# A new written-out order for a fused attention and FFN kernel: half tiles of their own for sequences 0 and 1, and the last output tile in two column halves

## The chip, the core and the metric

The kernel runs on one core of a Trainium2 chip. The core has five engines with instruction queues of their own: TensorE (PE, matrix products, with weight loads shown as PEld), VectorE (DVE), ScalarE (ACT), GpSimd (POOL) and SyncE (SP). They run side by side and wait for each other by semaphores only. Loads from HBM are issued by POOL, stores and transposes by DMA by SP. The metric is the device time of one execution in microseconds; smaller is better.

## The reference

Eight sequences of 576 positions, eight heads of 64. Keys and values are averaged over groups of 8 positions (72 remain), attention runs over these, and a gated FFN with a convolution over three positions follows. Cut to what is computed:

```python
k_p = k.reshape(B, H, Sp, pool, D).mean(axis=3)          # pool 8: 576 -> 72
v_p = v.reshape(B, H, Sp, pool, D).mean(axis=3)
scores = scale * np.matmul(q, k_p.transpose(0, 1, 3, 2))
scores = scores - np.max(scores, axis=-1, keepdims=True)
attn = np.exp(scores)
attn = attn / (np.sum(attn, axis=-1, keepdims=True) + 1e-09)
x = np.matmul(attn, v_p)  # -> (8, 576, 512), heads side by side
h = np.maximum(x @ w_in, 0.0)                            # 512 -> 1024
conv_out[s] = sum(conv_w[k] * h[s + k - 1] for k in range(3))
gate = 1.0 / (1.0 + np.exp(-conv_out))
out = (h * gate) @ w_out                                 # 1024 -> 512, float32
```

## The kernel before

The sequences are paired into four groups, [0, 1], [2, 3], [4, 5], [6, 7]. A sequence's 576 positions are 4 tiles of 128 and a half tile of 64. A group therefore has nine attention tiles: t = 0 to 3 of its first sequence, t = 5 to 8 of its second, and t = 4, whose 128 rows are the two half tiles together (`parts`, L479). So t = 4 needs keys, queries and values of both sequences, and both FFNs need t = 4 (`need`, L1045).

An attention tile passes through these steps: scores on PE (`att_scores`), the maximum over each head on DVE (`att_max`, L529), its subtraction (`att_shift`: for group 0 two PE matmuls into the same PSUM banks, L549; for the others a DVE addition, L541), the exponential on ACT (L567), the transpose of the exponentials (groups 0 and 1: five PE transposes, L578, and a copy, L592; groups 2 and 3: `att_send`, a DMA transpose issued by SP), the product with the values on PE (`att_values`, L603), the division on DVE (`att_divide`, L616 and L618), and the transpose into xT (groups 0 and 1 by PE and a copy, L635 and L643; groups 2 and 3 by a DMA transpose from SP, `att_out`).

The FFN of a sequence: eight blocks of 128 features through w_in (`ffn_in`, two halves of four matmuls each, L648) with a relu on ACT (L657); sequence 0 alone goes tile by tile (`ffn_in_tile`, L669). Then four convolutions of two blocks each, as products with diagonal matrices in quarters of the array (`ffn_conv`, L730, 64 or 80 matmuls), a tanh on ACT (L741), the gate on DVE (L752 to L759). Nine output tiles per group (`ffn_out`, L764, two steps of four matmuls of 512 columns), each copied out of PSUM (`ffn_copy`, L775) by DVE or ACT and stored by two DMAs of 64 rows (`ffn_store`, L787).

Before the attention of a sequence its q, k and v are loaded by POOL (`load_q`, L251; `load_k`, L251; `load_pair`, L258; `load_v`, L269 and L272), keys are pooled and queries transposed on PE, values pooled on DVE. Constants are made at the start: the pooling matrix (cleared by DVE, L310 to L312, cut out by POOL, L299, doubled by DVE, L315), the identity, the head mask (POOL, L318 and L320), its wide form (DVE, L337), cleared buffers (DVE, L295), and the first Exp, which brings ACT's table in (`start_exp`, L290 and L291). PE runs matmuls on a blank tile ("fills", L367) where the order has a spare.

Each such step is an operation of a graph (`add`) with the engines that can do it, what it comes after, and the buffers ("tokens") that it uses. The numbers given to `add` (durations, keys, landing times, counts) served a planner and emit nothing. What runs is the written order: `order` (L138) goes through ORDER, where n // 2 names the operation and n % 2 the engine, −1 is a fill, FORMS picks the array form (full, halves or quarters) and PLACES the PSUM banks. The other buffers are handed out in rotation (L149 to L151):

```python
                elif k.slots is None:
                    i = taken[k.ring] = taken.get(k.ring, -1) + 1
                    k.slots = [i % self.rings[k.ring]]
```

Every engine's queue holds its operations in that order.

Of the kernel before, what the change touches and what calls it, by code (L numbers as in the profile page):

```python
# [12 lines left out]
ACT = mybir.ActivationFunctionType  # L13
# [20 lines left out]
class Graph:  # L34
# [20 lines left out]
    X_DMA = 4  # L55
    SHIFT_DVE = 1
# [53 lines left out]
    )  # L110
    FORMS = (
        0, 0, 1, 1, 0, 1, 1, 1, 0, 0, 0, 0, 0, 1, 1, 0, 1, 0, 0, 0, 0, 0, 0, 0, 0, 1, 0, 0, 0, 1, 0, 1, 0, 1, 1, 1, 1, 1, 1, 1,
        0, 0, 0, 0, 0, 0, 0, 0, 1, 0, 1, 0,
    )
    PLACES = (
# [22 lines left out]
    def order(self):  # L138
        forms, places, spares, taken, done, seen = iter(self.FORMS), iter(self.PLACES), list(self.spares), {}, [], set()
        for n in self.ORDER:  # L140
# [4 lines left out]
            for k in o.uses:  # L145
# [14 lines left out]
def kernel(  # L160
# [10 lines left out]
    nc = tc.nc  # L171
# [985 lines left out]
```

## Time and profile before

| | us |
|---|---|
| median of 3 runs | 236.06 (235.92 to 236.71) |
| the profiled execution | 237.85 |
| its span, first to last instruction | 235.6 |
| PE busy in the span | 216.2 |
| DVE busy | 173.9 |
| ACT busy | 146.3 |
| POOL busy | 28.0 |
| mean granted TensorE clock | 0.98 of full speed |

The span is what the profile shows; the execution's own time is 2.25 longer. A busy share is a mean over stages, and the stages differ: loads at the start, attention and FFN mixed in the middle, output matmuls at the end. Groups of instructions are written as line, engine, operation, output<-inputs, count, busy time, mean duration, and idle time ahead of them with what ended it.

### The profile page before, as it was taken

What the parts mean: (1) busy time and instruction counts of PE and PEld (TensorE: products, weight loads), DVE (VectorE), ACT (ScalarE), POOL (GpSimd) and SP (SyncE); (2) the same over time, 40 slices, a digit from 0 to 9 for tenths busy, and PEclk for the clock granted to TensorE, in tenths of its full rate; (3) what the DMA queues carried; (4) which work ended last, traced back from release to release, by engine and by line L of the source; (5) the groups of instructions that cost most, each with busy time, mean ns of one, the idle gap of its engine ahead of it and who ended that gap; (6) DMA issues with size and microseconds to landing.
All of it is one profiled execution on the core that took longest, in us unless ns stands there. A gap on an engine that the chain in (4) does not pass through costs nothing. (4 is left out here: it accounts for less than half of the span.)

```text
span 235.6 us, 7790 instructions
## 1 busy us (share of the span) xinstructions
PE 216.2 (92%) x3362; PEld 150.8 (64%) x3362; DVE 173.9 (74%) x365; ACT 146.3 (62%) x246; POOL 28.0 (12%) x45
## 2 busy tenths in 40 slices
PE   6697899969999899988998899899999999999991
PEld 2455799756678777556764477568766665875440
DVE  4489886996999999988799779769757625716510
ACT  2245668896888997749766576358434563685320
POOL 7930731110000520300000000000000000000000
PEclk9979999997999999999999999999999999999998
DMA  5999999999940299999135777656665642601596
GB/s 88 163 186 207 207 207 207 207 207 206 191 98 3 19 199 185 230 179 171 25 70 32 155 150 137 130 124 132 91 133 116 130 85 46 136 3 38 112 203 143
DMA packets 44006, 31.51 MB, mean 134 GB/s; under 512 B 23596, under 2 KB 39364, under 8 KB 43972
## 3 DMA queue, kind: packets, MB, share of 16 engines
q0 software_dynamic: 16288, 16.26, 42.9%
q1 hardware_dynamic: 27604, 14.64, 32.3%
q8 instruction: 26, 0.43, 0.8%
q10 hardware_dynamic: 80, 0.13, 0.1%
q14 instruction: 8, 0.07, 0.1%
HBM read 32.52 MB, written 9.44 MB: 178 GB/s over the span
## 5 line engine op out<-in xcount | busy, mean ns | idle before, releaser
L764 PE MATMUL psum<-w_out_sb,gT 128*128 128x512 bf16 x288 | 70.2, 382 | 0.0
L648 PE MATMUL psum<-xT,w_in_sb 128*128 128x288 bf16 x448 | 63.7, 286 | 2.3 <-ACT tg L741 2.3
L648 PEld LDWEIGHTS <-w_in_sb 128*128 128x128 bf16 x448 | 42.0, 98 | 16.5 <-issue 2.8
L657 ACT ACTIVATE hT<-psum 128x576 bf16<-128x576 f32 x56 | 35.0, 649 | 23.8 <-PE psum L648 23.6
L741 ACT ACTIVATE tg<-psum 128x576 bf16<-128x576 f32 x64 | 37.5, 652 | 12.5 <-PE psum L730 11.0
L764 PEld LDWEIGHTS <-gT 128*128 128x128 bf16 x288 | 27.0, 98 | 25.4 <-issue 0.7
L529 DVE TENSOR_REDUCE negm<-psum 128x8 f32<-128x576 f32 (+1 forms) x36 | 27.1, 752 | 5.8 <-PE psum L516 3.9
L730 PE MATMUL psum<-hT,dw 64*64 64x288 bf16 (+4 forms) x1152 | 30.3, 246 | 1.1 <-ACT eT L592 0.3
L730 PEld LDWEIGHTS <-dw 64*64 64x64 bf16 x1152 | 25.3, 107 | 8.0 <-issue 7.3
L618 DVE TENSOR_TENSOR x<-psum,r 128x512 bf16<-128x512 f32 x36 | 24.9, 692 | 1.2
L775 ACT COPY osb<-psum 128x512 f32<-128x512 f32 (+1 forms) x26 | 14.6, 581 | 16.9 <-PE psum L764 15.1
L759 DVE TENSOR_TENSOR gT<-gT,hT 128x1152 bf16<-128x1152 bf16 x32 | 24.3, 758 | 1.1
L567 ACT ACTIVATE e<-sd 128x576 bf16<-128x576 f32 x27 | 18.2, 684 | 7.9 <-DVE sd L541 4.9
L775 DVE COPY osb<-psum 128x512 f32<-128x512 f32 (+1 forms) x11 | 7.3, 667 | 19.9 <-PE psum L764 14.5
L541 DVE TENSOR_TENSOR sd<-psum,negm 128x576 f32<-128x576 f32 x27 | 20.4, 755 | 0.8
L755 DVE TENSOR_SCALAR gT<-tg 64x576 bf16<-64x576 bf16 x64 | 19.7, 309 | 1.5 <-ACT tg L741 0.2
L603 PE MATMUL psum<-vm,eT 128*128 128x130 bf16 (+5 forms) x240 | 18.4, 222 | 1.4 <-DVE negm L529 1.4
L752 DVE TENSOR_SCALAR gT<-tg 128x576 bf16<-128x576 bf16 x32 | 9.5, 305 | 11.7 <-ACT tg L741 11.6
L603 PEld LDWEIGHTS <-eT 128*128 128x128 bf16 (+1 forms) x240 | 14.5, 100 | 4.3 <-DMA eT<-e 1.5
L434 DVE TENSOR_TENSOR v<-v 128x1280 bf16<-128x1280 bf16 (+2 forms) x24 | 13.0, 542 | 0.2
L592 ACT COPY eT<-psum 128x640 bf16<-128x640 bf16 x15 | 10.3, 691 | 4.4 <-PE psum L578 4.1
L616 DVE RECIPROCAL r<-psum 128x8 f32<-128x8 f32 x36 | 7.3, 202 | 7.8 <-PE psum L603 7.6
(73 smaller groups left out, 205.9 us busy)
## 6 DMA issues: line engine op xcount, KB each, us to landing
out_dram<-osb SPq DMA_DIRECT2D x71, 128.0 KB, 2.4
v<-in_v_dram POOLq DMA_DIRECT2D x8, 512.0 KB, 18.5
qp<-in_q_dram POOLq DMA_DIRECT2D x7, 576.0 KB, 14.0
kk<-in_k_dram POOLq DMA_DIRECT2D x3, 1152.0 KB, 13.9
w_in_sb<-in_moe_w_in_dram POOLq DMA_DIRECT2D x2, 512.0 KB, 17.0
w_out_sb<-in_moe_w_out_dram POOLq DMA_DIRECT2D x1, 1024.0 KB, 20.0
kk<-in_k_dram POOLq DMA_DIRECT2D x2, 288.0 KB, 4.5
kk<-in_k_dram POOLq DMA_DIRECT2D x1, 576.0 KB, 12.8
```

Source lines behind the costliest of these rows:

```text
L529: nc.vector.tensor_reduce(out=a["m"][0:rows], in_=a["s"][0:rows, :, 0:2 * KW].rearrange("p a (h s) -> p a h s", s=Sp), axis=AX.X, op=OP.ma ...
L541: nc.vector.tensor_tensor(out=a["d"][0:rows], in0=a["s"][0:rows, :, 0:2 * KW].rearrange("p a (h s) -> p a h s", s=Sp), in1=a["m"][0:rows]. ...
L603: nc.tensor.matmul(out=a["o"][lo:hi, h // 4, (h % 4) * (D + 1):(h % 4 + x1 - x0) * (D + 1)], lhsT=a["eT"][:, j, lo:hi], rhs=buf("vm", b)[: ...
L618: nc.vector.tensor_tensor(out=a["x"][0:rows].rearrange("p (a h d) -> p a h d", a=2, d=D), in0=ov[:, :, :, 0:D], in1=r[0:rows].unsqueeze(3) ...
L648: nc.tensor.matmul(out=banks(ps)[:, j, 0:SC], lhsT=w_in_block(dc, fb), rhs=buf("xT", g)[:, dc, i * S + j * SC:i * S + (j + 1) * SC], start ...
L657: nc.scalar.activation(out=buf("hT", b)[:, fb, :].rearrange("p (a s) -> p a s", a=2), in_=banks(ps)[:, :, 0:SC], func=ACT.Relu, scale=0.5,)
L730: nc.tensor.matmul(out=banks(pss[r ^ c])[c * D:(c + 1) * D, j, lo:hi], lhsT=dw[r * D:(r + 1) * D, tap * n_fb + fb, :], rhs=hT[r * D:(r + 1 ...
L741: nc.scalar.activation(out=tg.rearrange("p (a s) -> p a s", a=2), in_=banks(ps)[:, :, 0:SC], func=ACT.Tanh, scale=0.5,)
L755: nc.vector.tensor_scalar(out=gate[r * D:(r + 1) * D, fb], in0=tg[(1 - r) * D:(2 - r) * D], scalar1=1.0, scalar2=None, op0=OP.add)
L759: nc.vector.tensor_tensor(out=gate[:, both], in0=gate[:, both], in1=buf("hT", b)[:, both], op=OP.mult)
L764: nc.tensor.matmul(out=bank(ps)[0:rows, :], lhsT=buf("gT", g)[:, fb, t * P:t * P + rows], rhs=w_out_sb[:, fb, :], start=(fb == 0), stop=(f ...
L775: copy(out=osb[0:rows, columns], in_=bank(ps)[0:rows, columns])
```

## The change

Group 0 is named in `APART`: its t = 4 is now the half tile of sequence 0 alone, and a new t = 9 is the half tile of sequence 1, written to its own columns of xT (`columns_of`). The FFN of sequence 0 needs tiles 0 to 4, that of sequence 1 tiles 5 to 9. Ten attention tiles instead of nine are run in group 0. Output tile t = 4 still has both halves.

The last output tile (sequence 7, t = 8) is computed in two column halves of eight matmuls of 256 columns, each into a PSUM bank of its own; each half is copied and stored by two DMAs of 64 rows by 256 columns as soon as it is there (the first half's both from SP, the second's from SP and ACT).

ORDER, FORMS and PLACES are replaced, and PLACES now names the buffers of all rings. Some of the planner's numbers change. Read out of the lists:

| stretch | before | after |
|---|---|---|
| POOL at the start | k of 0 (2 loads), identity, pooling matrix, q of 0 (2), q 1, v 0, k 1, head mask, q 2, w_in (2), v 1, k of 2 and 3, q 3, w_out, q 4, v 2, v 3, v 4, q 5, k of 4 and 5 | k of 0 (2), head mask, identity, pooling matrix, q of 0 (2), v 0, k 1, q 1, q 2, w_in first half, v 1, w_in second half, k of 2 and 3, q 3, q 4, w_out, v 2, v 3, v 4, k of 4 and 5, q 6, q 7, q 5 |
| fills | 17 ahead of the first keys, then 5 and 3 | 4 ahead of the first keys, then 1, 1 and 1 |
| `start_exp` | first on DVE and ACT | amid the attention of group 1 |
| mask columns, wide mask, pick matrix | behind the first maxima | ahead of the first maximum |
| convolutions of sequence 0 (pairs of blocks) | 2, 1, 3, 0, two query preparations between | 1, 0, 2, 3, two query preparations between |
| first output matmuls | (0, t=2), behind all of PE's attention work for sequence 1 | (0, t=1), ahead of the values of (0, t=5) and the transposes back of t = 5, 6, 7 |
| end of PE | ..., (3, 5) second step, (3, 8) first, (3, 8) second | ..., (3, 5) second step, (3, 4) first, half 0 of (3, 8), (3, 4) second, half 1 of (3, 8) |
| end of SP | (3, 6), (3, 4), (3, 7), (3, 5), one half of (3, 8) | (3, 6), (3, 7), (3, 5), half 0 of (3, 8) twice, (3, 4) twice, one store of half 1 |

The diff, cut:

```diff
+    APART = (0,)
...
     ORDER = (
...
-        forms, places, spares, taken, done, seen = iter(self.FORMS), iter(self.PLACES), list(self.spares), {}, [], set()
+        forms, places, spares, done, seen = iter(self.FORMS), iter(self.PLACES), list(self.spares), [], set()
...
-                if k.slots is None and k.ring == "ps":
+                if k.slots is None:
                     i = next(places)
                     k.slots = list(range(i, i + k.n))
-                elif k.slots is None:
-                    i = taken[k.ring] = taken.get(k.ring, -1) + 1
-                    k.slots = [i % self.rings[k.ring]]
...
+        if t == 4 and g in Graph.APART:
+            return [(0, TB, bs[0])]
         if t == 4:
             return [(i * TB, (i + 1) * TB, b) for i, b in enumerate(bs)]
-        return [(0, P, bs[1])]
+        return [(0, TB if t == 9 else P, bs[1])]
+
+    def columns_of(g, t):
+        first = 4 * P + TB if t == 9 else t * P
+        return slice(first, first + rows_of(g, t))
...
-            out=buf("xT", g)[:, :, t * P:t * P + rows], in_=att[g, t]["x"][0:rows, :]
+            out=buf("xT", g)[:, :, columns_of(g, t)], in_=att[g, t]["x"][0:rows, :]
...
+    def half_columns(x):
+        return slice(x * d_model // 2, (x + 1) * d_model // 2)
+
+    def ffn_out(g, t, fbs, ps, columns=slice(0, d_model)):
+        rows = P
+        for fb in fbs:
...
-                    out=out[b].rearrange("(p c) d -> c p d", c=C)[c],
-                    in_=osb[j * TB:(j + 1) * TB, :],
+                    out=out[b].rearrange("(p c) d -> c p d", c=C)[c, :, columns],
+                    in_=osb[j * TB:(j + 1) * TB, columns],
...
-    LATE = 2.0
+    LATE = 1.8
...
-    c1 = add({"DVE": 0.6}, soon(), clear_pool_matrix)
+    c1 = add({"DVE": 1.5}, soon(), clear_pool_matrix)
...
-            o = add({"SP": 1.29}, key, lambda: att_send(g, t), after=[o, ze], uses=[e, eT], land=(1.7, 0, 1))
+            o = add({"SP": 1.29}, key, lambda: att_send(g, t), after=[o, ze], uses=[e, eT], land=(2.1, 0, 1))
...
-        need = [xdone[g, t] for t in range(5)] if i == 0 else [xdone[g, t] for t in range(4, 9)]
+        need = [xdone[g, t] for t in (range(5) if i == 0 else range(5, 10) if g in Graph.APART else range(4, 9))]
...
+            if b == B - 1 and n == len(n_outs[b]) - 1:
+                o = None
+                for x in range(2):
+                    sm = token("ps")
+                    o = add(pe(*[P * 2] * 8), key + x, lambda t=t, x=x, sm=sm: ffn_out(g, t, range(n_fb), sm, half_columns(x)),
+                            after=need + [wout, o], uses=[sm, gtok[g]], mode=FULL, count=16)
+                    c = add(either(0.42, 0.38), key + x, None, after=[o], uses=[osb, sm])
+                    c.emit = lambda c=c, t=t, x=x, sm=sm: ffn_copy(g, t, sm, copier(c), half_columns(x))
+                    for r, (e, queue) in enumerate((("SP", nc.sync), ("ACT" if x else "SP", nc.scalar if x else nc.sync))):
+                        add({e: 0.59}, key + x, lambda t=t, x=x, r=r, queue=queue: ffn_store(g, t, queue, r, half_columns(x)),
+                            after=[c], uses=[osb], land=(2.0, 0, 1))
+                continue
...
-            if b == B - 1 and n == len(n_outs[b]) - 1:
-                o = [add(d, key, lambda t=t, sm=sm, x=x, copy=copy: ffn_copy(g, t, sm, copy, slice(x * P * 2, (x + 1) * P * 2)),
-                         after=[o], uses=[osb, sm])
-                     for x, (d, copy) in enumerate(((dve(0.4), nc.vector.tensor_copy), (act(0.4), nc.scalar.copy)))]
-                for x, (e, queue) in enumerate((("SP", nc.sync), ("ACT", nc.scalar))):
-                    add({e: 0.59}, key, lambda t=t, x=x, queue=queue: ffn_store(g, t, queue, x), after=o, uses=[osb], land=(2.0, 0, 1))
-                continue
```

More of the change, by code (lines that the diff above doesn't have):

```diff
@@ L642, in att_copy_out @@
         rows = rows_of(g, t)
-        copy(out=buf("xT", g)[:, :, t * P:t * P + rows], in_=att[g, t]["xps"][:, 0:n_dmc, 0:rows])
+        copy(out=buf("xT", g)[:, :, columns_of(g, t)], in_=att[g, t]["xps"][:, 0:n_dmc, 0:rows])
     def ffn_in(b, fb, j, ps):
@@ L759, in ffn_gate @@
         nc.vector.tensor_tensor(out=gate[:, both], in0=gate[:, both], in1=buf("hT", b)[:, both], op=OP.mult)
-    def ffn_out(g, t, j, ps):
-        rows = rows_of(g, t)
-        for fb in range(n_fb // 2 * j, n_fb // 2 * (j + 1)):
+    def half_columns(x):
[3 more added lines that the diff above has]
+        for fb in fbs:
             nc.tensor.matmul(
-                out=bank(ps)[0:rows, :],
+                out=bank(ps)[0:rows, columns],
                 lhsT=buf("gT", g)[:, fb, t * P:t * P + rows],
-                rhs=w_out_sb[:, fb, :],
+                rhs=w_out_sb[:, fb, columns],
                 start=(fb == 0),
@@ L772, in ffn_copy, with ffn_store @@
     def ffn_copy(g, t, ps, copy, columns=slice(0, d_model)):
-        rows = rows_of(g, t)
+        rows = P
         osb = buf("osb", g, t)
         copy(out=osb[0:rows, columns], in_=bank(ps)[0:rows, columns])
-    def ffn_store(g, t, queue, only=None):
+    def ffn_store(g, t, queue, only=None, columns=slice(0, d_model)):
         osb = buf("osb", g, t)
@@ L813 @@
     FULL, HALF, QUARTER = (128, 128), (128, 64), (64, 64)
-    n_tiles = {b: [t for t in range(9 if len(groups[g]) == 2 else 5) if (t < 5) == (i == 0)]
-               for b, (g, i) in where.items()}
+    n_tiles = {b: [t for t in range(10 if g in Graph.APART else 9) if (t < 5) == (i == 0)] for b, (g, i) in where.items()}
     n_outs = {b: list(range(5)) if len(groups[g]) == 1 else [t for t in range(9) if (t < 4) == (i == 0)]
@@ L891, in add_load_pair @@
         loads["kk", g] = add({"POOL": 0.65}, key, lambda: load_pair(g), uses=[kk[g]], land=(LATE, 2 * kb, RATE))
-    picked = add({"DVE": 0.5}, START + Graph.DW - 1, build_pick, after=[c0])
+    picked = add({"DVE": 0.95}, START + Graph.DW - 1, build_pick, after=[c0])
     for b in (1, 2, 3):
@@ L1027, in add_att @@
         if b0 >= Graph.X_DMA:
-            o = add({"SP": 1.29}, key, lambda: att_out(g, t), after=[o], uses=[x, xtok[g]], land=(1.7, 0, 1))
+            o = add({"SP": 1.29}, key, lambda: att_out(g, t), after=[o], uses=[x, xtok[g]], land=(2.1, 0, 1))
         else:
@@ L1083, in add_out @@
         for n, t in enumerate(n_outs[b]):
-            rows = rows_of(g, t)
             key = w + 3 * rounds[n] - 1 + Graph.OUT + (Graph.LAST if b == B - 2 else 0) if b < B - 1 else w + n
             key += nudge("ot", 9 * g + t)
-            sm, osb = token("ps"), token("osb", g, t)
+            osb = token("osb", g, t)
+            need = [a for x in groups[g][0:i + 1] for a in gdone[x]]
+            if b == B - 1 and n == len(n_outs[b]) - 1:
[10 more added lines that the diff above has]
+                continue
@@ L1088, in add_out @@
+            sm = token("ps")
             o = None
             for j in range(2):
-                need = [a for x in groups[g][0:i + 1] for a in gdone[x]]
-                o = add(pe(*[512] * 4), key, lambda t=t, j=j, sm=sm: ffn_out(g, t, j, sm), after=need + [wout, o],
-                        uses=[sm, gtok[g]], mode=FULL if rows == P else HALF, count=8)
-            if b == B - 1 and n == len(n_outs[b]) - 1:
-                o = [add(d, key, lambda t=t, sm=sm, x=x, copy=copy: ffn_copy(g, t, sm, copy, slice(x * P * 2, (x + 1) * P * 2)),
-                         after=[o], uses=[osb, sm])
-                     for x, (d, copy) in enumerate(((dve(0.4), nc.vector.tensor_copy), (act(0.4), nc.scalar.copy)))]
-                for x, (e, queue) in enumerate((("SP", nc.sync), ("ACT", nc.scalar))):
-                    add({e: 0.59}, key, lambda t=t, x=x, queue=queue: ffn_store(g, t, queue, x), after=o, uses=[osb], land=(2.0, 0, 1))
-                continue
+                o = add(pe(*[512] * 4), key, lambda t=t, j=j, sm=sm: ffn_out(g, t, range(4 * j, 4 * j + 4), sm), after=need + [wout, o],
+                        uses=[sm, gtok[g]], mode=FULL, count=8)
```

14 lines of the change are left out of this document (7 added, 7 removed), and 125 rows, old and new, of tables (ORDER, PLACES).

## The prediction

> **What bounds the kernel now.** I read the page's busy shares first, then stage by stage the table of windows, then what ends PE's idle times, and last the timeline around them and the tail.
>
> ```profile
> span 235.6 us, 7790 instructions
> PE 216.2 (92%) x3362; PEld 150.8 (64%) x3362; DVE 173.9 (74%) x365; ACT 146.3 (62%) x246; POOL 28.0 (12%) x45
> ```
>
> The windows (us, then each engine's busy time, TensorE's granted clock, DMA share, GB/s):
>
> ```profile
> 0.00:8.00 8.00, 6.18 (x49) 2.95 (x51) 2.42 (x13) 1.71 (x3) 6.75 (x15) 1.00 0.65 93
> 8.00:11.50 3.50, 1.95 (x35) 1.27 (x30) 2.17 (x8) 1.28 (x5) 3.36 (x7) 1.00 1.31 193
> 11.50:15.00 3.50, 3.06 (x26) 1.63 (x26) 3.46 (x12) 1.94 (x3) 2.18 (x4) 0.51 1.17 182
> 15.00:28.00 13.00, 10.38 (x276) 7.81 (x275) 11.78 (x21) 7.04 (x12) 3.97 (x6) 1.00 1.22 204
> ...
> 42.00:50.00 8.00, 7.23 (x231) 5.46 (x219) 7.71 (x18) 7.04 (x13) 0.76 (x1) 1.00 1.23 208
> 50.00:52.00 2.00, 0.40 (x6) 0.14 (x4) 1.89 (x7) 1.81 (x5) 1.01 (x1) 1.00 1.24 204
> 52.00:56.00 4.00, 4.00 (x49) 2.94 (x49) 2.22 (x3) 2.31 (x4) 0.00 (x0) 0.57 1.24 207
> 56.00:100.00 44.00, 42.90 (x686) 32.05 (x688) 42.23 (x79) 37.59 (x64) 6.46 (x9) 1.00 0.82 137
> 100.00:122.00 22.00, 20.07 (x413) 14.99 (x402) 19.44 (x45) 15.76 (x27) 0.00 (x0) 1.00 0.72 108
> 122.00:152.00 30.00, 27.46 (x384) 17.99 (x383) 25.31 (x45) 18.24 (x30) 0.00 (x0) 1.00 0.69 123
> 152.00:231.00 79.00, 78.77 (x984) 50.58 (x982) 44.71 (x99) 41.23 (x71) 0.00 (x0) 1.00 0.51 105
> ```
>
> From 152 us PE never rests: the time is settled earlier. Up to 28 us DVE sets the pace (11.78 of 13.0) with loads arriving at 204 GB/s; 42 to 52 is DVE and ACT; 56 to 100 has PE and DVE both above 95%. The dear stops of PE (the wait in brackets stands ahead of the named matmul; the first is followed by half clock, the 0.57 above), and the tail:
>
> ```profile
> 51.76 0.29 PE L635 MATMUL psum<-ident,x 128*128 128x128 bf16 x2 [1.60 <-issue]
> ...
> 106.90 0.28 PE L648 MATMUL psum<-xT,w_in_sb 128*128 128x288 bf16 x1 [1.76 <-ACT tg L741]
> ...
> 130.19 0.55 PE L603 MATMUL psum<-vm,eT 128*64 128x130 bf16 x12 [1.36 <-DVE negm L529]
> ...
> 230.92 0.42 DVE L775 COPY osb<-psum 128x256 f32<-128x256 f32 x1 [3.68 <-PE psum L764]
> 231.38 0.37 ACT L775 COPY osb<-psum 128x256 f32<-128x256 f32 x1 [1.61 <-DVE osb L775]
> 231.78 0.56 ACTq L787 DMA_DIRECT2D out_dram<-osb  x1
> ```
>
> PE ends at 230.84, DVE and ACT copy the two halves of the last tile one behind the other, the last stores start at 231.78 and the span closes 3.84 later.
>
> **Work.** An attention tile more in group 0. PE: scores 0.25, shift 0.25, five transposes 0.28, four back 0.23, two value groups (0.31 each, estimated from 0.36 for a full tile) for one of 0.53; one q preparation in quarters (0.41) for halves (0.63): +1.0 us. Below, "work" is each order's list with every group at its median time from start to next start (0.86 for four output matmuls, 0.49 for four of w_in, 0.87 to 0.91 for a convolution, and so on), fills left out: 199.0 us for PE before, 200.0 after. DVE: 0.75 + 0.20 + 0.69, with swapped copies +1.8; ACT +2.2. The planner's numbers (LATE, costs, counts) emit nothing: 0. Buffers are now picked from a written list instead of in rotation; that moves waits, has no row, and lies inside the bounds of the middle. The Exp warm-up now comes late; its table load (1.28 us) then stands before ACT's first copy, where ACT idled 5.5 us: 0.
>
> **Start.** POOL builds the head mask (0.17 + two of 0.24, some 0.75 with gaps) before identity and pooling matrix, and it had no gap there: q of sequence 0 is issued at 5.75 instead of 4.98 and, at 4.4 us to landing, lands near 10.1 instead of 9.36. The first maximum (11.13 before, 1.8 after that landing) comes near 12.0. In return the mask columns (0.49), the wide mask (1.14), the kT clears (1.2), the pick matrix (0.40) and part of v's clears move into DVE's idle first 10 us. From that maximum to the second maximum of sequence 1 DVE had 16.6 us of work and took 16.64; it now has 14.6: 26.6. PE adds shift 0.35, values 0.31, q preparation 0.6, scores 0.25, and I allow 0.5 for gaps: the first tile of w_in (L669) starts at 28.6 (27.91 before). PE has 185.8 us left there, 186.8 before: **−0.3**, between −0.8 (no gaps) and +0.5 (no DVE gain). v of sequence 0 and k of 1 land some 2 to 3 us sooner, q of 1 later; w_in's second half lands near 33 instead of 29.4, and 5.0 us of PE work lie between the first FFN tile and its first use: covered, by little.
>
> Of the fills 18 go. The first 17 kept PE busy to 7.05 although keys (5.54) and matrix (5.40) were there, so the key preparation can start 0.8 sooner; next it waits for q anyway: 0. But the clock rows: 8 to 11.5 with PE 56% busy is followed by half clock to 14.9, and five fills then carried PE through; now there is one fill there. A half-clock window of 3.4 us costs at most 1.7; behind DVE I take 0 here and price it as a rival. The Trainium skill's page "TensorE: Matmul & The Clock Gate" (The HAM clock gate) speaks against dropping fills: the array starts at half clock and is released only by a busy 3.4 us window, whose phase differs by run. By that rule the sum would be up to 1.7 us higher for each window that stays cold; the trace agrees as far as half clock there lasts 3.4 us (11.5 to 14.9).
>
> **42 to 56 us.** Sequence 0's FFN no longer needs anything of sequence 1. From its first convolution ACT had, to the last tanh, 8.2 us (among it an exp and the copy of a transpose), then gates, and the first output matmul came 12.4 us after the convolution (42.12 to 54.51). In the new order ACT's list to the last tanh is 8 x 0.65, two q copies 1.12, one pair copy 0.4: 7.9, after 0.95 of convolution; last gate 1.4: 10.3. Convolutions start at 28.6 + 12.1 of work + 0.7 (before: 14.2 us for 13.6 of work) = 41.4, outputs at 51.7, with 166.8 left (165.6 before): 218.5 against 220.1, so another **−1.3**. w_out, now behind q of 4, lands near 49.5 (45.9): in time. PE still has 3.4 us slack in those 10.3, so the 1.60 stop ("issue", no semaphore; PE's code arrives by the same busy DMA engines) hides if it recurs, but a clock window may go cold again. Before, half clock lasted to 55.9, 1.4 us behind that start: **−0.7** if it doesn't, 0 if it does.
>
> **Middle.** To the last convolution of sequence 2, PE has 67.2 us of work and DVE 73.6 (before 61.5 and 68.0 in 67.66 us). At that pace it ends at 51.7 + 73.9 = 125.6 with 99.6 left: 225.2, where before it was 122.17 + 104.0 = 226.2, which would give back 1.3 of the 2.3. Without the known stops (0.69, 0.26, 1.76 and the cold 0.7) PE would take 70.2 and gain 2.4 more; DVE's durations overlap a little (173.9 busy for 184.2 summed, 0.944); 73.6 x 0.944 / 0.97 (the share it reached in 60 to 100) is 71.6, its bound. I take 73.1, between that bound and the old pace and nearer the pace (new stops come for old ones, and q of 6 and 7, now loaded before 70 us, keep the DMA engines that also bring PE's code full some 5 us longer): 224.4, a give-back of **+0.5**, ends +1.3 and −2.4.
>
> **From 122 us.** Transposes by DMA take 2.9 us to landing (eT), 2.5 (xT). PE work planned between issue and use was 1.0, 2.3, 3.2 us at the tightest for eT; the 1.36 stop is the one with 2.3. Now the tightest are 3.2, 3.7, 3.8. For xT it was 0.0, 0.2, 0.5 and is 3.1 at least. The stops here sum to 2.5 (1.36, 0.50, 0.43, 0.25): I take **−0.9**, ends −2.5 and +1.
>
> **Tail.** Second halves need one copy after PE instead of two, 0.4 less. But SP's stores take about 0.6 each, and behind the last matmul SP still has both stores of the tile before (copy done 0.1 before PE's end): free at +1.2, where the last store started at +0.94 before. Smaller landing: **0**, ends −0.4 and +0.3.
>
> Sum −0.3 −1.3 −0.7 +0.5 −0.9 = −2.7. The profiled execution took 237.85 (span 235.6, 2.25 around it); the median is 236.06. **233.4 us.**
>
> **Rivals.** *DVE paces all up to 122 us* (its 1.8 us more are paid): no gain of DVE at the start (+0.5 for −0.3), the old pace in the middle (1.0 left of the gains up to there), half of the stops behind 122 us (−0.4): −1.0 + 0.8 − 0.4 = −0.6, 235.5. For it: 42.23 of 44 us; against: PE was as full, and DVE's first 8 us were 70% empty. *The start stays cold* (slower): without the fills two or three windows more between 8 and 28 us run at half clock, the matmuls between DVE's steps take twice as long, and DVE waits for PE instead of the reverse. Two windows cost 3.4, three 5.1, if nothing hides them: 236.8 to 238.5, I take 237.5. It decides from 3.4 us unhidden, which is the forecast's 2.7 and the 0.7 of a measurable change. For it: the 0.51 row, behind a stretch 56% busy. Against: half clock makes PE busier, which releases it, and 2.6 of 13 us are spare in 15 to 28. The rule of the Trainium skill's page "TensorE: Matmul & The Clock Gate" is this rival; the trace's one window behind a thin stretch bears it out in part. *All known stops go*: −0.3 −1.3 −0.7 with the middle at DVE's bound (71.6: 123.3 + 99.6 = 222.9, 1.0 less) and 2.1 of the 2.5 behind 122 us: −5.4, 230.7. For it: the transposes' new margins; against: an order that long has never met the chip without some stop, 7.4 us of them from 28 us on in the one before.
>
> **Numbers.** Forecast 0.52 (231.9 to 235.2), DVE's pace 0.16 (234.9 to 236.4), cold 0.19, all stops 0.13. A measurement of this kernel tells some 0.3% (0.7 us) from no change. Faster: 0.50 + 0.05 + 0.13 = 0.68; same: 0.02 + 0.09 + 0.01 = 0.12; slower: 0.02 + 0.18 = 0.20. 230.4 to 237.4 leaves out the upper half of the cold case and the edge of the fourth, some 0.15.
>
> **What would show it.** First w_in matmul near 28.6; first output matmul near 52, with no half-clock window between 50 and 56; last convolution of sequence 2 near 124.5; no stop above 0.5 us of value matmuls behind a transpose; the last store issued about 1.2 us after PE's end. Wrong if half clock covers more than two windows before 28 us, if the first output matmul comes after 54, or if DVE is at 98% and PE below 92% from 56 to 120.

## The result, and the profile after

The changed kernel takes **233.99 us** (median of 4 runs, 232.68 to 236.91) against 235.99 of the kernel before on the same chip: ratio **0.9871** (95% interval 0.9822 to 0.9919). The ratio leaves out the longest of the four (236.91), which counts as a slow run; the two medians as they stand give 0.9915. Forecast was 233.4, so 0.989. In a second series on another chip the same kernel, run again, took 234.30 against 236.95, ratio 0.9888 (0.9833 to 0.9944). It is faster, by 2 to 3 us, a little over 1%.

The first profiled execution was the slowest of its four, so the lines here are those of the second series ("again", 235.91 us, span 234.1); its line numbers are 32 to 35 above those of the kernel before (first w_in tile L701, w_in L680, convolution L762, output L799). First the busy shares, then the windows, with the same columns as in the prediction:

```profile
span 234.1 us, 7843 instructions
PE 213.0 (91%) x3365; PEld 151.7 (65%) x3385; DVE 175.0 (75%) x369; ACT 146.7 (63%) x248; POOL 27.9 (12%) x45
```

```profile
0.00:8.00 8.00, 3.27 (x24) 1.62 (x26) 5.75 (x26) 1.28 (x1) 6.61 (x16) 1.00 0.55 78
8.00:11.50 3.50, 1.98 (x25) 1.27 (x27) 1.26 (x2) 0.47 (x2) 3.50 (x6) 1.00 1.31 165
15.00:28.00 13.00, 11.06 (x258) 8.03 (x254) 11.19 (x23) 9.32 (x16) 4.18 (x5) 1.00 1.22 208
...
42.00:50.00 8.00, 7.72 (x210) 6.28 (x208) 7.74 (x18) 7.71 (x13) 1.60 (x2) 1.00 1.24 207
50.00:52.00 2.00, 1.27 (x24) 1.11 (x25) 1.91 (x6) 1.99 (x5) 0.78 (x1) 1.00 1.24 206
52.00:56.00 4.00, 3.27 (x79) 2.02 (x77) 3.92 (x7) 3.67 (x6) 1.48 (x2) 1.00 1.24 206
56.00:100.00 44.00, 43.21 (x733) 32.88 (x735) 42.41 (x82) 38.55 (x70) 4.94 (x7) 1.00 0.97 156
100.00:122.00 22.00, 20.06 (x411) 14.45 (x410) 19.07 (x39) 13.82 (x23) 0.00 (x0) 1.00 0.62 87
122.00:152.00 30.00, 28.60 (x344) 19.50 (x348) 26.52 (x54) 19.80 (x35) 0.00 (x0) 1.00 0.61 112
```

DVE is no longer 70% empty in the first 8 us (5.75 instead of 2.42), and in 50 to 56 PE works at full clock, at smaller matmuls (103 in place of 55). From 56 to 100 PE and DVE stand as before. The 1.00 ahead of 16.7 us says nothing: the clock's first record stands there, and the matmuls ahead of it ran at half speed (below). PE's dearest stops now, and the tail:

```profile
28.76 0.38 PE L494 MATMUL psum<-ident,qp 64*64 64x64 bf16 x24 [0.88 <-issue]
50.60 0.27 PE L667 MATMUL psum<-ident,x 64*128 64x64 bf16 x4 [0.63 <-ACT qT L500]
104.75 0.75 PE L762 MATMUL psum<-hT,dw 64*64 64x160 bf16 x28 [1.30 <-issue]
128.65 1.63 PE L680 MATMUL psum<-xT,w_in_sb 128*128 128x288 bf16 x12 [1.03 <-ACT tg L773]
...
229.42 0.42 DVE L810 COPY osb<-psum 128x256 f32<-128x256 f32 x1 [0.18 <-PE psum L799]
229.87 0.57 ACTq L822 DMA_DIRECT2D out_dram<-osb  x1
```

The stops of 1.60 at 50 and 1.36 at 129 are gone; new ones stand at 28, 103 and 127.6. ("issue" means that nothing in the profile released PE; the section "PE's code" finds the reason.) In the tail one copy follows PE's end (229.32) instead of two.

**Where the time went.** The same four marks in every execution, in us. "Queries" is the landing of the first load of q of sequence 0; "rest" is the execution's own time less PE's end.

| execution | queries | first w_in | queries to w_in | w_in to first output | first output to PE's end | rest |
|---|---|---|---|---|---|---|
| before | 9.36 | 27.91 | 18.55 | 26.60 | 176.32 | 7.02 |
| changed, first profile | 10.88 | 30.63 | 19.75 | 22.31 | 177.38 | 6.59 |
| again | 11.21 | 30.92 | 19.71 | 22.16 | 176.24 | 6.59 |
| predicted | 10.1 | 28.6 | 18.5 | 23.1 | 176.4 | 7.0 |

The whole gain lies between the first w_in matmul and the first output (4.3 to 4.4 us), and up to 3 us of it is paid back by a later start. The experiments ask what each of these is.

The granted clock of every execution is on record too, and it says where a part of the gain comes from. On the second chip, the longest (240.69) left out, 10 of 16 executions of the kernel before had a mean clock of 0.981 to 0.993, which is room for a half-clock window of 3.41 us (0.007), and took 237.4 us in the mean; the other six, at 0.994 or more, took 235.9. The six of the changed kernel there all had 0.995 or more and took 234.3. (Half clock ahead of a trace's first clock record is not in these means.) So some 0.9 us of the gain seems to be half clock that no longer comes, and some 1.6 us is there without it.

### The profile page after: what moved, and what is told of

Its sections match the earlier page's. It is cut to its first block, busy times and chain, and to the rows that moved or that the text cites. A ratio compares the mean times of both kernels' runs of the same rounds, so it can differ in the third digit from the quotient of the medians.

```text
span 235.1 us, 7863 instructions
## 1 busy us (share of the span) xinstructions
PE 214.9 (91%) x3385; PEld 151.6 (64%) x3385; DVE 174.9 (74%) x369; ACT 146.6 (62%) x248; POOL 27.8 (12%) x45
## 4 chain that ended last, share of the span: by engine, by line
PE 66%; DVE 14%; DMA 5%; ACT 5%; issue 4%; POOL 2%; SPq 1%; DVEq 0%; ACTq 0%; POOLq 0%
PE psum L780 25%; PE psum L661 18%; PE psum L743 8%; PE psum L616 4%; PE psum L682 3%; DVE x L631 3%; PE psum L529 2%; DMA qp<-in_q_dram 2%; DMA xT<-x 2%; DVE gT L772 2%; ACT tg L754 2%; PE psum L591 2%; DVE kk L413 2%; DVE gT L768 2%; DVE negm L542 1%
## 5 line engine op out<-in xcount | busy, mean ns | idle before, releaser
L780 PE MATMUL psum<-w_out_sb,gT 128*128 128x512 bf16 (+1 forms) x296 | 69.4, 374 | 1.3 <-ACT osb L791 0.9
L661 PE MATMUL psum<-xT,w_in_sb 128*128 128x288 bf16 x448 | 62.8, 286 | 2.1 <-DMA xT<-x 1.2
L670 ACT ACTIVATE hT<-psum 128x576 bf16<-128x576 f32 x56 | 34.4, 649 | 20.3 <-PE psum L661 20.3
L542 DVE TENSOR_REDUCE negm<-psum 128x8 f32<-128x576 f32 (+2 forms) x37 | 27.5, 752 | 5.3 <-PE psum L516 3.1
L631 DVE TENSOR_TENSOR x<-psum,r 128x512 bf16<-128x512 f32 (+1 forms) x37 | 25.6, 691 | 1.3
L616 PE MATMUL psum<-vm,eT 128*128 128x130 bf16 (+5 forms) x240 | 19.0, 222 | 0.7 <-DVE vm L445 0.5
L616 PEld LDWEIGHTS <-eT 128*128 128x128 bf16 (+1 forms) x240 | 15.4, 100 | 4.5 <-issue 1.3
L629 DVE RECIPROCAL r<-psum 128x8 f32<-128x8 f32 (+1 forms) x37 | 7.5, 202 | 12.5 <-PE psum L616 12.4
L481 ACT COPY qT<-psum 128x1152 bf16<-128x1152 bf16 (+1 forms) x11 | 11.8, 1071 | 3.0 <-PE psum L471 2.1
## 6 DMA issues: line engine op xcount, KB each, us to landing
v<-in_v_dram POOLq DMA_DIRECT2D x8, 512.0 KB, 16.7
```

The lines of the kernel that those rows point to most:

```text
L542: nc.vector.tensor_reduce(out=a["m"][0:rows], in_=a["s"][0:rows, :, 0:2 * KW].rearrange("p a (h s) -> p a h s", s=Sp), axis=AX.X, op=OP.ma ...
L616: nc.tensor.matmul(out=a["o"][lo:hi, h // 4, (h % 4) * (D + 1):(h % 4 + x1 - x0) * (D + 1)], lhsT=a["eT"][:, j, lo:hi], rhs=buf("vm", b)[: ...
L631: nc.vector.tensor_tensor(out=a["x"][0:rows].rearrange("p (a h d) -> p a h d", a=2, d=D), in0=ov[:, :, :, 0:D], in1=r[0:rows].unsqueeze(3) ...
L661: nc.tensor.matmul(out=banks(ps)[:, j, 0:SC], lhsT=w_in_block(dc, fb), rhs=buf("xT", g)[:, dc, i * S + j * SC:i * S + (j + 1) * SC], start ...
L670: nc.scalar.activation(out=buf("hT", b)[:, fb, :].rearrange("p (a s) -> p a s", a=2), in_=banks(ps)[:, :, 0:SC], func=ACT.Relu, scale=0.5,)
L780: nc.tensor.matmul(out=bank(ps)[0:rows, columns], lhsT=buf("gT", g)[:, fb, t * P:t * P + rows], rhs=w_out_sb[:, fb, columns], start=(fb == 0),
```

## Experiments

All edits are made to the changed kernel unless said otherwise. Ratios are to the kernel before on the same chip, so that the kernel as changed is 0.987 to 0.989.

### The same kernel again

> The changed kernel once more, for a profile of an ordinary execution (the one on hand took 236.91 us, the slowest of four). If the late start of that profile belongs to the kernel (TensorE at half clock until 16.5 us, first maximum at 13.2, first w_in matmul at 30.6), it is here again within 0.5 us, and the time is 233 to 235. If it belonged to that execution, the first w_in matmul starts near the forecast's 28.6 and the span is 231 or less. The two PE stops that nothing in the profile releases (0.91 us at instruction 766 of PE, 1.56 us at 3579) stand at the same instruction numbers if they are fetches of PE's code in blocks of 256 instructions, whatever their length; if they are chance, they stand elsewhere.

0.9888 (0.9833 to 0.9944). The late start is there again: first maximum at 13.52, first w_in matmul at 30.92. But in other kernels below with the same start it came at 28.11 to 29.89; here PE's transposing of the first queries, in this execution and then in that of "tail_act":

```profile
11.26 1.06 PE L490 MATMUL psum<-ident,qp 128*64 128x128 bf16 x16 [1.52 <-DMA qp<-in_q_dram]
```

```profile
9.84 0.64 PE L490 MATMUL psum<-ident,qp 128*64 128x128 bf16 x16 [0.69 <-DMA qp<-in_q_dram]
```

Two things differ: the queries landed 1.4 us later, though they were issued at 5.79 and 5.74, and the same 16 matmuls took 1.06 instead of 0.64, half clock against full. The stops without a releaser stand after the same number of PE instructions as in the first profile.

### Nine more fills

```diff
+ DVE: blank tile cleared first
+ PE: 7 fills ahead of the first key preparation, 2 behind the second
```

> Nine more fills: the blank tile is cleared first on DVE, and seven fills stand ahead of the first key preparation, two between the second and the query preparation. Theory 1 (a cold TensorE sets the start): half clock ends near 8 to 12 us instead of 16.5, the key and query preparations take 0.76 instead of 1.29, the first maximum comes 0.3 to 0.8 sooner, the first w_in matmul 1.0 to 1.5 sooner (near 29.3), and the time is 1.0 to 1.5 us lower than the changed kernel's. Theory 2 (DVE and the landing of the queries set the start): the clock is full sooner, the first maximum moves by less than 0.3, and so does the time. Code blocks: with 18 PE instructions more ahead, the unexplained PE stops move to the same multiples of 256 in PE's count, so 18 instructions earlier in the program.

0.9915 (0.9884 to 0.9947): no gain. In its profile full clock is there from 4.23 to 127.11 us, queries land at 9.78, and the first w_in matmul starts at 28.42, 18.64 behind them: by this mark 1.1 us of the 2.5 come from the clock and 1.4 from the queries' landing. The gain is still there at the last tanh of sequence 2 (126.41 instead of 128.51), and is lost at the stop behind it:

```profile
127.03 3.24 PE L682 MATMUL psum<-xT,w_in_sb 128*128 128x288 bf16 x13 [1.53 <-ACT e L601]
```

```profile
123.70:127.11 3.41, 1.78 (x51) 1.27 (x42) 3.31 (x7) 3.17 (x6) 0.00 (x0) 1.00 0.80 81
127.11:130.52 3.41, 3.41 (x15) 2.08 (x15) 2.86 (x7) 0.45 (x1) 0.00 (x0) 0.50 0.67 137
```

With PE busy for 1.78 of 3.41 us, the next 3.41 run at half clock, 1.7 us of work lost. So theory 1 is right on the start and was wrong on the time. Only for the profiled execution, the longest of the 12, is this the reason: its mean clock is 0.988, and the 0.994 to 1.000 of the other 11 has no room for such a window. They took 234.0 to 236.0 us all the same; where their gain went is not shown.

### The head mask behind the queries

```diff
- POOL: keys (2 loads), head mask, identity, pooling matrix, q of 0 (2 loads)
+ POOL: keys (2 loads), identity, pooling matrix, q of 0 (2 loads), head mask
- DVE: v cleared, then pooling matrix
+ DVE: pooling matrix cleared, then v
```

> POOL builds the head mask after the two loads of the queries of sequence 0, as before the change, and DVE clears the pooling matrix sooner. Theory 1 (the landing of the queries is the chain): they are issued some 0.7 us sooner, land near 10.2 instead of 10.9, and first maximum, first w_in matmul and time come 0.5 to 0.7 us sooner. Theory 2 (the cold array or DVE's list sets the start): the landing moves and the first w_in matmul does not, time within 0.3 us of the changed kernel.

0.9886 (0.9842 to 0.9931), no difference in time to the kernel as changed. In the trace the queries go out at 5.00, land at 9.41, and the first w_in matmul starts at 28.72, 19.31 behind them with half clock up to 12.4. The landing moves the start (theory 1); the 0.7 is smaller than what executions differ by.

### SP's queue at the 127 us stop

```diff
- SP: stores (0,5), stores (0,6), transposes of x (2,4), (2,0)
+ SP: transposes of x (2,0), (2,4), stores (0,5), stores (0,6)
```

> SP issues the transposes of x of tiles (2,0) and (2,4) ahead of the stores of output tiles (0,5) and (0,6), where they stood behind them. Theory 1 (SP's queue made sequence 4's first w_in matmuls wait: x was divided at 117.6 us, the transpose was issued at 124.2 and landed at 128.8): the PE stop of 1.24 us near 127.7 is gone and the time falls by 0.8 to 1.2. Theory 2 (the transpose's own landing is the wait, or PE's next stop takes its place): the stop moves and the time changes by less than 0.3.

SP's queue as changed ("again"), and in this kernel, then PE there:

```profile
118.13 2.38 SPq L619 DMA_TRANSPOSE eT<-e  x1
120.56 2.50 SPq L822 DMA_DIRECT2D out_dram<-osb  x4
123.16 4.75 SPq L659 DMA_TRANSPOSE xT<-x  x3
```

```profile
117.05 2.04 SPq L619 DMA_TRANSPOSE eT<-e  x1
119.18 2.53 SPq L659 DMA_TRANSPOSE xT<-x  x2
121.76 2.51 SPq L822 DMA_DIRECT2D out_dram<-osb  x4
...
126.10 0.44 PE L548 MATMUL psum<-kT,qT 128*64 128x144 bf16 x8
126.47 3.60 PE L680 MATMUL psum<-xT,w_in_sb 128*128 128x288 bf16 x28
```

The stop is gone: sequence 4's w_in matmuls follow the scores at once. From the last tanh of sequence 2 to that of sequence 4 it takes 32.1 us instead of 33.1 to 33.4, and from the first w_in matmul to PE's end 197.5, against 198.4 to 199.7 for the kernels with SP's old order and no half clock there. Theory 1. The time (0.9860, 0.9810 to 0.9910) shows the 1.0 only within its interval.

### The half tiles alone, in the old order

The kernel before, with `APART`, `columns_of` and ten attention tiles in group 0, but with its own order and its own last tile. In the first version the half tile of sequence 0 stands in one row behind the other tiles of that sequence:

```diff
+ scores (0,4), maximum, shift, exponential, transposes, copy, values, division, transposes back, copy:
+   one behind the other, between the divisions of sequence 0 and the first w_in tile
- the joint tile (0,4)
+ the half tile (0,9) in its place
```

> The old order and the old last tile, with the half tiles split alone: the half tile of sequence 1 takes the place of the joint tile, the half tile of sequence 0 is put ahead of it, behind the attention of the other tiles of sequence 0. Theory 1 (the split costs an attention tile, and only the new order turns it into a gain): PE has 1.0 us more, DVE 1.8, ACT 2.2, all in the stretch up to 56 us that DVE and ACT pace; the first w_in matmul comes 1 to 2 us later than in the kernel before, and the time is 0.5 to 1.8 us above it. Theory 2 (the split frees the FFN of sequence 0 by itself): the first output matmul comes sooner than 54.5 and the time is below the kernel before by 0.5 or more.

1.0245 (1.0206 to 1.0284), 5.3 us **slower** than the kernel before: the first w_in matmul starts at 33.48, and the two stretches behind it (26.12 and 175.61) are no longer than before. As the steps stand in one row, PE waits at each for DVE or ACT (1.93, 0.61 and 0.67 us in the profile), and two half-clock windows lie there too (25.55 to 32.38 us). A second version spreads them between the steps of tiles 1 and 2:

> The old order and the old last tile with the half tiles split alone, as before, but the steps of the half tile of sequence 0 are spread between those of the tiles t = 1 and t = 2 of that sequence, so that PE finds other work between them. Theory 1 (the 5.6 us of the first version came from the place of the steps): the first w_in matmul comes 1 to 2.5 us later than in the kernel before, near the 1.0 us of PE and 1.8 of DVE that the split adds, and the time is 1 to 2.5 us above it. Theory 2 (the split costs far more than its work wherever it stands in the old order): again 4 us or more.

1.0277 (1.0221 to 1.0332). Again the start takes it all: 32.50, though queries landed at 9.55. First PE's wait for the half tile's maximum, then the window behind it:

```profile
21.72 0.40 PE L566 MATMUL psum<-negm,ident 64*64 64x288 bf16 x2 [0.97 <-DVE negm L546]
```

```profile
22.26:25.68 3.42, 3.42 (x27) 2.50 (x26) 0.97 (x3) 0.94 (x2) 0.00 (x0) 0.50 1.24 207
```

From the first maximum to the first w_in matmul DVE has 1.7 us more (17.16 busy instead of 15.51), PE waits 0.97 for it and 1.33 at 30.55 for a division, and a half-clock window follows the first, up to 1.7 more. Theory 2, for these two places; that no place in the old order is cheaper isn't shown. So the split by itself gained nothing here, and with the new order it is part of a gain. That the order pays because it empties DVE's list first (mask, wide mask, clears and pick matrix in its idle first 10 us) is an argument from the lists: no run moves these alone, and none has the new order without the split.

### The first outputs late

```diff
  PE: ... transposes back (0,7), (0,5)
+     first output tile (0,1), first step of (0,2)      (moved from ahead of values (0,5))
```

> The changed kernel with its first output tile (0, t=1) and the first step of (0, t=2) moved behind the transposes back of sequence 1 (t=7 and t=5), as the old order had its first outputs. Theory 1 (the early outputs fill PE while the attention of sequence 1 waits for ACT and DVE): PE loses up to 2.6 us of cover (three steps of 0.86), the stretch from the first w_in matmul to the first relu of sequence 1 grows by 1 to 2.6 us, and so does the time. Theory 2 (DVE or ACT paces that stretch, and the gain came from the independence of the half tile alone): the stretch and the time stay within 0.4 of the changed kernel.

1.0074 (1.0033 to 1.0115): the gain is gone, and more. The profile (its shortest execution) had the warm, early start, 28.35:

```profile
51.53 0.48 PE L494 MATMUL psum<-ident,qp 64*64 64x64 bf16 x36 [1.33 <-ACT qT L500]
```

```profile
50.00:53.39 3.39, 1.49 (x63) 1.12 (x61) 3.32 (x6) 3.08 (x5) 1.72 (x3) 1.00 1.24 204
53.39:56.80 3.41, 3.02 (x28) 2.50 (x27) 3.18 (x7) 2.93 (x5) 0.53 (x1) 0.50 1.24 205
```

Without the outputs PE has 1.49 us of work in 3.39, DVE 3.32 and ACT 3.08; then half clock, as in the kernel before. To the last tanh of sequence 1 it takes 58.5 us from the first w_in matmul, where all the kernels with early outputs take 55.4 to 55.8 and the kernel before 59.4; to the first relu of sequence 1, the mark of the two theories, it is 36.1 instead of 33.0 to 33.4. Theory 1, with the clock on top of the lost cover: three output steps (2.6 us) are worth 3.1 here in the profile, and 4.4 to 4.8 by the ratios. The mean clock is 0.980 to 0.993 in all 12 executions, so each has room for a half-clock window.

### The tail

```diff
- last tile: half 0 (8 matmuls of 256 columns), half 1, a copy and two stores each
+ last tile: two steps of 4 matmuls of 512, DVE and ACT copy a half each, one store from SP, one from ACT
```

> The new order with the last output tile as it was: two steps of four matmuls of 512 columns at the places of the two halves, DVE and ACT copy a half each, SP and ACT store 64 rows each over the full width. Theory 1 (the halves pay nothing because SP still has both stores of the tile before): from PE's end to the span's end stays 4.8 us within 0.3, and the time within 0.3 of the changed kernel. Theory 2 (the halves pay): that stretch and the time are 0.4 to 0.8 longer.

0.9952 (0.9921 to 0.9983). The rest behind PE's end is 7.16 us instead of 6.59: theory 2, the halves pay 0.57 in the new order. The ratio is further off, 1.5 to 1.9 us above the changed kernel's, with intervals that overlap or nearly meet; what the rest would be is not shown. The second edit:

```diff
- SP: both stores of (3,4)
+ SP: first store of (3,4); ACT: second store of (3,4)
```

> The second store of output tile (3,4) goes out on ACT's queue instead of SP's. Theory 1 (SP's queue holds the last store back): the last store from SP starts 0.5 to 0.6 sooner after PE's end (0.6 instead of 1.2), and the stretch from PE's end to the span's end falls from 4.8 to 4.2 or 4.3. Theory 2 (the copy by ACT and its own store, or the landing of the bytes, set the end): the stretch stays within 0.2 of 4.8.

0.9907 (0.9875 to 0.9940). The last SP store starts 0.77 behind PE's end instead of 1.40 and lands at 3.26 instead of 3.51; the rest is 6.35, 0.24 less. Both theories have a part: SP frees 0.6, but 0.4 of it goes into the landing, perhaps since the stores then overlap. In the time the 0.24 doesn't show.

### Four edits together

> Four edits together: nine more fills, the head mask after the queries of sequence 0, SP's transposes of x ahead of the two stores, the second store of tile (3,4) from ACT. If the start is queries plus a warm array, the stop near 127 is SP's order and the tail is SP's queue, the gains add: queries land near 9.4, the first w_in matmul starts 18.6 us later (28.0), the stop near 127 is gone with no cold window behind it, the tail is 0.5 shorter, and the time is 2 to 3 us below the changed kernel. If something else (DVE in the middle, PE's code) takes the gains back, the first w_in matmul comes sooner all the same and the time is within 1 us of the changed kernel's.

0.9892 (0.9850 to 0.9933): **no better** than the kernel as changed. The parts do what they did alone: first w_in matmul at 28.40, 18.46 behind the queries (which took 4.95 us to land this time), no stop at 127, a rest of 6.28. But from the first w_in matmul to PE's end it is 199.0 again, with the stop at 101 grown to 1.62 and a new one of 0.72 at 146, on another transpose of x. The second theory, for the time. No version tried beats the changed kernel by more than these runs can tell.

### PE's code

The "issue" stops stand, in every kernel whose records are complete, behind 351, 863 or 1757 matmuls, counted from the start with the fills, whatever the order: 863 in the kernel before and in both half-tile kernels, 351 and 1757 in the changed one. With a weight load for each matmul, 1024 instructions lie between the first two, 4 times 256, and 1788 between the last two, 4 short of 7 times 256. If 64 more instructions stand ahead of the first matmul (this number is fitted), the stops come at 2.99, 6.99 and 13.98 times 256. (A convolution is 32 or 40 matmuls in the profile; the 64 or 80 named above count the weight loads too.) The page counts the loading:

```profile
q8 instruction: 26, 0.43, 0.7%
```

0.43 MB in 26 packets is 16 KB each. At each of the 24 "issue" stops of 0.6 us or more in these 14 profiles, whatever its length (0.88 to 2.47 us), PE starts again 1.26 to 1.49 us after the end of one and the same packet: the second of the 26 for the stop behind 351 matmuls, the sixth for 863, the thirteenth for 1757. So these stops wait for PE's instructions. In the kernel before, a packet starts about when the block two before its own is used up: 2.2 to 3.6 us later for the first seven, under full load, and at most 1.3 us later from 112 us on. The count is not exact: in the changed kernel some packets start up to 2.3 us ahead of it. The test moves the blocks, with 64-column fills where PE has no work:

```diff
+ DVE: blank tile cleared first
+ PE: 36 fills of 64 columns ahead of the first key preparation
```

> The changed kernel with the blank tile cleared first and 36 more fills of 64 columns each ahead of the first key preparation, where PE has nothing to do. They add 72 PE instructions and nothing else, so each boundary between blocks of 256 PE instructions lies 72 instructions earlier in the program. Theory 1 (PE's code comes in blocks of 256, the block after next is fetched only when a block is used up, and a block that runs in less than some 5.4 us makes PE stop): by the times of an execution of the changed kernel the short blocks are now 2.9 us (from 19.9), 4.9 (from 43.0), 3.7 (from 96.1) and 4.6 (from 99.8); PE stops without a releaser near 23, 48, 100 and 104 us, for some 2, 0.5, 1.7 and 0.8 us, where the changed kernel stopped for 0.9 at 27.6 and 1.1 to 1.6 at 103; the time is 1 to 3 us above the run with nine more fills, less what DVE's pace hides of the first stop. Theory 2 (these stops belong to the place in the program): they stay at the same instructions of the program, and the time stays within 0.5 of that run.

1.0214 (1.0156 to 1.0272): some 7 us more than with nine fills, from 36 tiny matmuls where PE stood idle.

```profile
27.77 0.22 PE L502 MATMUL psum<-ident,qp 64*64 64x64 bf16 x4 [2.47 <-issue]
53.33 0.29 PE L675 MATMUL psum<-ident,x 64*128 64x64 bf16 x4 [1.15 <-ACT tg L781]
107.42 0.54 PE L502 MATMUL psum<-ident,qp 64*64 64x64 bf16 x24 [2.30 <-issue]
```

```profile
28.95:32.37 3.42, 3.42 (x61) 2.47 (x60) 2.09 (x3) 2.16 (x4) 1.33 (x2) 0.50 1.24 207
107.46:110.87 3.41, 3.41 (x68) 2.23 (x68) 0.53 (x1) 2.31 (x3) 0.00 (x0) 0.50 0.45 131
```

The stops stay behind 351 and 1757 matmuls, so they moved 36 matmuls in the program (the last from amid a convolution into a query preparation), and they are 0.7 to 1.6 us longer than in the changed kernel's two profiles: theory 1. The one expected near 48 is doubtful: behind 863 matmuls PE waits for 1.15 us, but the profile puts it down to a tanh, and it ends 1.60 us after its packet. They come 2 to 5 us later than expected because the start was late and cold (half clock from 8.47 to 15.30, behind 3.41 us in which PE, with its 64-column fills, was busy for 1.39), and the fourth is missing. The cost was expected at 1 to 3. The two half-clock windows behind the stops add at most 3.4 to that and the cold start comes on top; in five of the six executions the mean clock is 0.966 to 0.975. How the 7 divide was not measured.

### Few fills in the old order

The kernel before, with fills cut from 17, 5 and 3 to 4, 2 and 1.

> The kernel before with 7 fills instead of 25: 4 ahead of the first keys, then 2 and 1. Theory 1 (without fills the array stays at half clock for most of the first 16 us): from the landing of the first queries to the first w_in matmul it takes 19.3 to 19.8 us, as in the cold starts of the changed kernel, instead of 18.55, and the time is 0.7 to 1.2 us above the kernel before. Theory 2 (DVE paces the start): 18.3 to 18.7, and the time within 0.4 of it.

1.0060 (1.0022 to 1.0097), 0.5 to 2.3 us slower, as theory 1 has it; but by its mark it is theory 2: half clock up to 16.55 us, and the first w_in matmul still 18.58 behind the queries (before 18.55), DVE busy for 15.54 of the 16.27 us ahead of it. In the old order DVE seems to hide the cold array there. Where the time went instead is open: the one profile, of its second longest execution, has a second half-clock window at 153 behind a stop of 1.38.

## Why the prediction was right

The time was 0.6 us off and the sign right. The chain that was forecast is the one that the profiles show, but that the sum came out so near is partly luck: the start came 0.9 us later than forecast in the mean of six executions, the first output 0.9 sooner behind it, and 0.35 was saved outside the span, for which the sum has no term. Step by step:

- **Start, −0.3: mis-sized.** The first w_in matmul was put at 28.6. In six executions with this start it came at 28.11, 28.35, 28.87, 29.89, 30.63 and 30.92, 29.5 in the mean. The chain was right: 18.31 to 18.61 behind the queries where full clock came by 9 us, as in the 18.5 of the forecast. Two terms were not: queries took 4.1 to 5.4 us to land, not 4.4, and the dropped fills, entered at 0, cost 0.7 to 1.2 (19.28 to 19.75 behind the queries) in the three executions that ran cold to 14.7 us or longer. In two of them half clock lasted to 16.5 and 16.7, which the prediction had named as a sign of its being wrong; the time held all the same, since the next stage gave more. That the cold array is the cost rests on this sorting of executions and on one profile with nine more fills (18.64).
- **The cold rival** had its mechanism, but not its price: 0.7 to 1.2 instead of 3.4 to 5.1. Up to the landing of the queries PE waits in any case (1.52 us in "again"). From there half clock lasted 5.5 us more in "again", with PE busy for 4.7 of them, so by estimate at most 2.4 us of work was lost, and about half of that doesn't show in the time; DVE's list is the likely cover, which no run tests by itself. Whether it happens differs by execution: full clock first came at 7.9 to 9.0 us in four of the six and at 16.5 and 16.7 in two. The Trainium skill's page "TensorE: Matmul & The Clock Gate" (The HAM clock gate) says that the window runs freely and is not tied to the kernel's start; the six starts agree with that.
- **42 to 56 us, −1.3 and −0.7: right, and larger.** First output 22.2 to 22.3 behind the first w_in matmul instead of 23.1: the convolutions came 12.6 to 12.7 behind it (12.8 forecast), the output 9.6 behind them instead of 10.3, since ACT's list to the last tanh took 7.2 us and not 7.9. The last link, "last gate 1.4", was wrong, and its fit is luck: the first output step reads blocks 0 to 3 alone, whose gates had ended at 49.71 in "again", and it started at 53.08, before the last gate ended (53.39). What released it is ACT's copy of a transpose (eT, ended at 53.03), so ACT's list paces the output to its end. No half-clock window followed. "late_out" shows that the early outputs carry most of this.
- **Middle and from 122 us, +0.5 and −0.9: right in sum.** From the first output to PE's end 176.4 was forecast; four executions with this order took 176.2 to 177.4. Inside, one reading failed: "xT is 3.1 at least". The margin counted PE's work between a transpose's issue and its use as if SP issued it when x was there. x of (2,0) was divided at 117.6 in the first profile, but SP had two other transposes and four stores to issue first and issued it at 124.2; it landed at 128.8. "sp_swap" shows it: with the transposes first the stop is gone. The new stops in place of old ones, which the middle allowed for, came, as a PE code block at 103.
- **DVE's pace** did not decide from 56 us on: up to 100 us PE is busy for 43.21 of 44 us beside DVE's 42.41.
- **Tail, 0: at its lower end.** From PE's end to the span's end 4.79 before and after, as forecast, with SP as the reason. But the time outside the span went from 2.25 to 1.8, which the prediction had held constant; 0.08 of the 0.43 is the landing of the last store (3.59 to 3.51 behind PE's end). The other 0.35 has no explained cause. It goes with the new order, and neither with the split nor with the last tile: 1.75 to 1.90 us lie outside the span in every kernel that has the new order, "tail_whole" with the old last tile among them, and 2.20 to 2.25 in every one with the old order.

## What to carry to other kernels

A split that removes a dependency costs its extra work at once; here it gained only together with an order that uses the freedom to fill an engine's waits, so try it without that order before believing in it. When a margin for a transfer is read from a plan, add what stands ahead of it in the issuing queue. And price a PE stop with what follows it: here a stop that left PE busy for half of a 3.4 us window or less was in many cases followed by half clock, and then cost its length and up to 1.7 us more.

## What the runs showed of the hardware

- **PE's instructions arrive by DMA in blocks of 256 while the kernel runs**, and a block that runs in 3 to 5 us, as rows of small transposes and convolutions do, can make PE stop for 0.9 to 2.5 us under "issue". It did not always: in the kernel before, a block that ran in 4.0 us near 125 us, with lighter DMA load, was followed by no stop. Adding or dropping a few matmuls anywhere ahead shifts all later boundaries: 36 of them at the start turned stops of 0.9 and 1.3 into 2.5 and 2.3, the second 100 us later.
- **Half clock needs no idle window.** Each stretch of half clock in these profiles that follows recorded full clock, up to PE's end, came behind 3.41 us in which PE was busy for 1.1 to 1.9 us: 1.81 in the kernel before at 52.45, 1.78 in "fills", 1.51 in "late_out", 1.10 and 1.11 in "pad36". The reverse holds only in part. With full clock cut into windows of 3.41 us from its start, all six windows with less than 1.6 us busy were followed by half clock, of the twelve with 1.65 to 1.9 only six were, and none with 1.95 or more. What decides between them is open.
- **The same load, issued at the same time, lands 4.0 to 5.4 us later**, execution by execution (the first of q of sequence 0, issued at 5.73 to 5.79 us in the kernels with the new order and the head mask first), and the first w_in matmul moves with it: there it came 18.3 to 18.6 us behind the landing wherever full clock came by 9 us and stayed.
